# Attention and gated MLP on one Trainium2 core: the order of all operations from a table instead of a greedy scheduler

## The chip, the core and the metric

The kernel runs on one core of a Trainium2 chip. The core has a matrix engine (TensorE, PE in the rows), a vector engine (VectorE, DVE), an engine for functions of one tensor (ScalarE, ACT), a general one (GpSimd, POOL) and a sync engine (SyncE, SP), which here issues all DMA transfers. Each takes its own queue of instructions in order and waits at the front of it for semaphores of the others. Loads of weights into PE (PEld) overlap its matmuls. The metric is the device time of one execution in microseconds (us), the median over runs.

## What is computed

Causal attention for 4 batches of 12 heads (448 positions, 64 wide), whose output goes as x into a gated MLP with a spatial mix. All inputs are float32, some weights arrive as 64-bit numbers.

```python
scores = (q @ k.transpose(0, 1, 3, 2)) / np.sqrt(64)
scores = np.where(mask, -1e9, scores)            # causal
attn = np.exp(scores - scores.max(-1, keepdims=True))
attn = attn / (attn.sum(-1, keepdims=True) + 1e-9)
x = (attn @ v).transpose(0, 2, 1, 3).reshape(4, 448, 768)
h = np.maximum(x @ w_in, 0)                      # 768 -> 1024
u, v = h[..., :512], h[..., 512:]
v_n = (v - mean(v)) / np.sqrt(var(v) + 1e-6)
v_s = np.einsum('ts,bsd->btd', w_spatial, v_n) + b_spatial[None, :, None]
out = (u * v_s) @ w_out                          # 512 -> 768
```

## The kernel before

The kernel first writes down all its work as a list of 2517 operations (`Plan.add`), each with the engines that may run it and a time on each, what it reads and writes, and the buffers it needs. Then `Plan.run` decides engine by engine in which order they are issued. The operations are these.

Attention goes by pairs of heads, 24 pairs, six to a batch, numbered from 0. For each pair `load` brings q and k in and `qk_prepare` brings them into the form in which the head's 64 rows lie on partitions: for the first twelve pairs by PE transposes in float32 (`qk_turn`, L708, copies L729 and L731), for the others scaled, split into two 16-bit halves (L528 is the second half, by subtraction) and turned by a DMA transpose into qkT (L773, L784). Scores go into PSUM banks ps (L859 for the first ten pairs, L1005 for two, L1015 and L1016 later), DVE adds the mask and takes the maximum (L884, L1026), ACT the exponential (L894, L1038), DVE sums and reciprocals (L905, L1052, L1060). The weights e are turned by PE (L933, copied to et by L958 and L960) or, from pair 10 on, by DMA transposes (L1142). The product with the values is L1167, into the one bank px, and leaves it through ACT (L1184) and DVE (L1189) into xT.

The MLP (`ffn`) goes by batches, once six pairs are done. All its matmuls are in `chain` (L1396), in pieces of three. It makes the v half of h (L1462), its norm (L1470 to L1508), the u half (L1545, L1547), the spatial product (L1577), g = u times v_s, in two halves (L492 to L496 and L1417), and the output (evacuated into buffers o by L1613 and L1615, stored by L1625).

The weights are prepared in between: `prep_in` for w_in (L1236 and `from_double`), `prep_sp` for w_spatial, `prep_out` for w_out. `prep_out` takes eight loads (L1362) into the two buffers o, which later also hold outputs. From each load `from_double` assembles 32-bit numbers in three steps on DVE (L1202, L1208, L1213), and then a rounded copy (L494 or L496) and the rest (L1376) are written into wo.

What sets the order: each engine takes the ready operation with the smallest rank. The rank is a latest start, worked back from due times (`DUE`) and shifted by two tables of offsets (`LEAN` by part and engine, `NUDGE` by group). `WHERE` says which engine runs an operation that several could. Where PE has nothing ready in the first 46 us of the plan, a filler matmul is issued, L660, which multiplies a constant into the bank pf2:

```python
if op is None:
    if e == "PE" and self.warm and 1300 <= now < WARM:
        order.append((self.warm, e))
        busy[e] = pe_end = now + FILL
```

Of the kernel before, what the change touches and what calls it, by code (L numbers as in the profile page):

```python
# [57 lines left out]
)  # L58
NUDGE = (
# [5 lines left out]
)  # L65
LEAN = {
    (0, "DVE"): -1630, (0, "PE"): 330, (0, "POOL"): -3560, (0, "SP"): 1020, (1, "ACT"): 5410, (1, "DVE"): -1290, (1,
    "PE"): 1970, (1, "POOL"): -4890, (1, "SP"): -5940, (2, "ACT"): -3040, (2, "PE"): 6920, (2, "POOL"): 610, (2,
    "SP"): 5090, (3, "DVE"): 21930, (3, "PE"): 8670, (3, "POOL"): 4350, (3, "SP"): 4620, (4, "ACT"): -25990, (4,
    "DVE"): -4700, (4, "SP"): 6360, (5, "ACT"): 360, (5, "DVE"): 16860, (5, "PE"): 1330, (5, "POOL"): 1940, (6,  # L70
    "ACT"): -5080, (6, "DVE"): -1250, (6, "PE"): -2420, (6, "POOL"): 1170, (6, "SP"): -5620, (7, "ACT"): -5140, (7,
    "DVE"): 830, (7, "PE"): -10610, (7, "POOL"): -2630, (7, "SP"): -120, (8, "ACT"): 1470, (8, "DVE"): 1160, (8,
    "PE"): 4610, (8, "POOL"): 1070, (9, "DVE"): -1240, (9, "PE"): 1950, (9, "POOL"): 4140, (9, "SP"): 1390, (10,
    "ACT"): -1730, (10, "DVE"): -1120, (10, "PE"): 410, (11, "ACT"): 1330, (11, "PE"): -580, (11, "POOL"): -3820,
    (11, "SP"): 200, (12, "ACT"): 60, (12, "DVE"): -180, (12, "PE"): 6160, (12, "POOL"): -2020, (13, "ACT"): 3270,
    (13, "DVE"): 560, (13, "PE"): -950, (13, "POOL"): -3310, (13, "SP"): 4100, (14, "DVE"): 3280, (14, "POOL"):
    1600, (14, "SP"): 330, (15, "ACT"): 490, (15, "DVE"): -1430, (15, "POOL"): -1560, (15, "SP"): -430, (16, "ACT"):
    -1470, (16, "DVE"): -2030, (16, "POOL"): -1090, (16, "SP"): -4720, (17, "ACT"): 2080, (17, "DVE"): 2600, (17,
    "PE"): 1720, (17, "POOL"): 4210, (17, "SP"): -450, (18, "ACT"): -1950, (18, "DVE"): -6170, (18, "PE"): -1700,
    (18, "POOL"): -550, (18, "SP"): -14920, (19, "ACT"): 1850, (19, "SP"): -4980, (20, "ACT"): 4940, (20, "DVE"):  # L80
    480, (20, "POOL"): 880, (20, "SP"): -4390, (21, "DVE"): 2620, (21, "POOL"): 3170, (22, "ACT"): 13050, (22,
    "DVE"): 590, (22, "PE"): -10700, (22, "POOL"): 280, (22, "SP"): -11070, (23, "ACT"): 5360, (23, "DVE"): -840,
    (23, "POOL"): 2610, (23, "SP"): -330, (24, "DVE"): 2330, (24, "PE"): 430, (24, "POOL"): 4180, (24, "SP"): -2720,
    (25, "ACT"): -11200, (25, "DVE"): -2770, (26, "ACT"): -6170, (26, "DVE"): -2660, (26, "PE"): 200, (26, "POOL"):
# [225 lines left out]
def kernel(  # L310
# [278 lines left out]
    st = {}  # L589
# [1110 lines left out]
```

## Time and profile before

| | |
|---|---|
| time, median of 3 runs | 380.98 us (380.76 to 385.32) |
| the profiled execution's own time | 383.96 us |
| its span, first to last instruction | 382.2 us |
| what lies around the span | 1.76 us |
| PE busy, fillers included | 364.3 us, 95% |
| DVE / ACT / POOL busy | 298.1 / 259.8 / 147.2 us |
| granted clock of TensorE, mean | 0.989 |

Busy time is the time in which an engine executes. [...] In a row of the timeline the time in brackets is how long the engine was idle just before, and behind the arrow stands what ended it. An instruction's line in the rows is a line of the kernel before.

### The profile page before, as it was taken

The numbers are of one execution on the slowest core, as the hardware profiler recorded it, in microseconds if no ns is written. First come the engines' busy times: TensorE is split into PE (matmuls) and PEld (weight loads), VectorE is DVE, ScalarE is ACT, GpSimd is POOL, SyncE is SP. The second block draws the span as 40 slices with busy tenths as digits, with TensorE's granted clock in tenths as the row PEclk, the third lists the DMA queues.
The fourth block names the chain that finished last, engine by engine and source line by source line (L and its number), as shares of the span: only waits on it lengthen the run. The fifth ranks groups of instructions, "written<-read, shape, count | busy, mean of one in ns | idle before, by whom it ended". The sixth has DMA issues, their size and how long they took to land.

```text
span 382.2 us, 8138 instructions
## 1 busy us (share of the span) xinstructions
PE 364.3 (95%) x2621; PEld 233.3 (61%) x2621; DVE 298.1 (78%) x1152; ACT 259.8 (68%) x764; POOL 147.2 (39%) x208
## 2 busy tenths in 40 slices
PE   8999999899999999699998989999899999999995
PEld 6676654456445554576654548865455687555695
DVE  4998989899899999669887889889799988154210
ACT  1889997689989594379886794787785579142111
POOL 3111496258985522023596041413163310034410
PEclk9999999999999999889999999999999999999999
DMA  7999953563325999928999989989657678600022
GB/s 189 229 228 229 219 123 121 149 121 96 88 49 132 236 216 207 234 101 160 192 204 171 188 140 144 232 191 202 139 115 138 107 171 152 147 0 0 2 82 82
DMA packets 157964, 56.64 MB, mean 148 GB/s; under 512 B 151457, under 2 KB 153698, under 8 KB 157922
## 3 DMA queue, kind: packets, MB, share of 16 engines
q1 hardware_dynamic: 157922, 56.14, 70.9%
q8 instruction: 20, 0.33, 0.4%
q14 instruction: 22, 0.18, 0.1%
HBM read 26.76 MB, written 5.51 MB: 84 GB/s over the span
## 4 chain that ended last, share of the span: by engine, by line
PE 46%; DVE 20%; ACT 16%; DMA 12%; issue 3%; SPq 2%; ACTq 0%; DVEq 0%
PE pf L1396 26%; PE px L1167 5%; ACT ps L1038 5%; PE pf L660 5%; PE ps L859 3%; DMA et<-e 3%; DMA o<-in_moe_w_out_dram 3%; DVE ps L1026 3%; ACT e L494 3%; ACT junk L572 2%; PE ps L933 2%; DVE e L1127 2%; DVE ps L884 2%; PE ps L708 2%; PE ps L1015 2%
## 5 line engine op out<-in xcount | busy, mean ns | idle before, releaser
L1038 ACT ACTIVATE ps<-ps,sm 128x384 f32<-128x384 f32 (+4 forms) x98 | 45.4, 464 | 24.1 <-DVE sm L1026 17.3
L1396 PE MATMUL pf<-wi,xT 128*128 128x512 f16 (+1 forms) x360 | 59.8, 337 | 0.0
L1396 PE MATMUL pf<-xT,wi 128*128 128x448 f16 x288 | 59.0, 352 | 0.1
L1396 PE MATMUL pf<-wo,g 128*128 128x384 f32 x288 | 57.0, 351 | 1.6 <-ACT o L1613 1.3
L1396 PEld LDWEIGHTS pf<-wo,g 128*128 128x128 f32 x288 | 51.9, 196 | 4.3 <-ACT o L1613 1.4
L1127 DVE SCALAR_TENSOR_TENSOR e<-ps,sm,e 128x256 f16<-128x256 f32 (+4 forms) x98 | 45.2, 505 | 5.4 <-ACT e L494 5.2
L1396 PEld LDWEIGHTS <-wi 128*128 128x128 f16 x288 | 27.8, 99 | 24.9 <-issue 1.4
L496 POOL TENSOR_SCALAR e<-e,sm 128x384 f32<-128x384 f32 (+3 forms) x38 | 22.7, 606 | 52.1 <-DVE sm L905 14.7
L494 ACT ACTIVATE e<-ps,sm 128x384 f16<-128x384 f32 (+4 forms) x98 | 40.9, 515 | 2.6 <-DVE sm L1060 2.6
L1396 PEld LDWEIGHTS <-xT 128*128 128x128 f16 (+1 forms) x360 | 27.7, 103 | 23.1 <-issue 3.6
L1026 DVE CUSTOM_DVE_ANT_0 ps<-ps,mask,sc 128x384 f32<-128x384 f32 (+4 forms) x84 | 38.3, 507 | 4.1 <-PE ps L1016 3.8
L894 ACT ACTIVATE e<-ps,sm 128x128 f32<-128x128 f32 (+3 forms) x70 | 34.0, 497 | 6.3 <-DVE sm L884 4.3
L1396 PE MATMUL pf<-wst,vn 128*128 128x448 f16 (+1 forms) x176 | 36.1, 353 | 0.0
L1489 POOL TENSOR_TENSOR ln<-ln,mhalf 128x1 f32<-128x1 f32 (+1 forms) x16 | 9.2, 588 | 56.5 <-DVE ln L1481 42.4
L859 PE MATMUL ps<-qkT 64*128 64x128 f32 (+3 forms) x160 | 27.7, 445 | 0.9 <-ACT e L894 0.9
L1396 PEld LDWEIGHTS <-vn 128*128 128x128 f16 (+1 forms) x176 | 16.8, 98 | 16.2 <-issue 1.3
L884 DVE CUSTOM_DVE_ANT_0 ps<-ps,e 128x256 f32<-128x256 f32 (+2 forms) x60 | 24.2, 441 | 2.7 <-PE ps L859 2.5
L933 PE MATMUL ps<-ident,e 128*128 128x128 f32 x160 | 23.8, 279 | 1.3 <-DVE qkT L731 0.9
L1167 PE MATMUL px<-et,vs 128*64 128x448 f16 (+3 forms) x336 | 22.7, 276 | 1.9 <-DMA et<-e 1.8
L1016 PE MATMUL ps<-qkT 128*64 128x384 f16 (+4 forms) x168 | 21.9, 285 | 1.5 <-DMA qkT<-qkT 1.5
L933 PEld LDWEIGHTS ps<-ident,e 128*128 128x128 f32 x160 | 17.6, 141 | 9.1 <-issue 4.0
L528 POOL TENSOR_TENSOR qks<-qk,qks 112x512 f16<-112x512 f32 x15 | 17.8, 1200 | 13.8 <-ACT qks L494 13.6
(152 smaller groups left out, 755.2 us busy)
## 6 DMA issues: line engine op xcount, KB each, us to landing
wb<-in_moe_w_in_dram SPq DMA_DIRECT2D x12, 512.0 KB, 4.6
vnat<-in_v_dram SPq DMA_DIRECT2D x24, 192.0 KB, 4.2
out_dram<-o SPq DMA_DIRECT2D x12, 384.0 KB, 2.6
o<-in_moe_w_out_dram SPq DMA_DIRECT2D x8, 384.0 KB, 4.2
qk<-in_q_dram SPq DMA_DIRECT2D x24, 112.0 KB, 4.2
qk<-in_k_dram SPq DMA_DIRECT2D x24, 112.0 KB, 3.9
qk<-in_q_dram SPq DMA_DIRECT2D x12, 224.0 KB, 3.9
qk<-in_k_dram SPq DMA_DIRECT2D x12, 224.0 KB, 4.0
```

The lines of the kernel that those rows point to most:

```text
L494: nc.scalar.activation(out=dst, in_=src, func=AF.Copy, scale=scale)
L496: nc.gpsimd.tensor_scalar(out=dst, in0=src, scalar1=scale, scalar2=1.0, op0=ALU.mult, op1=ALU.mult)
L859: nc.tensor.matmul(out=at(bank)[r0:r0 + rn, o0:o0 + n], lhsT=flat32(t)[rows, q0:q0 + rn], rhs=k32(t)[rows, :n], start=True, stop=True, ski ...
L884: lambda e, ps=ps, n=n, u=u0 + u, sm=sm, o0=o0, h=h: nc.vector.tensor_tensor_reduce(out=at(ps)[:, o0:o0 + n], in0=at(ps)[:, o0:o0 + n], in ...
L894: lambda e, ps=ps, n=n, u=u0 + u, sm=sm, o0=o0, c=c: nc.scalar.activation(out=at(eb)[:, 128 * c:128 * c + n], in_=at(ps)[:, o0:o0 + n], fu ...
L933: nc.tensor.transpose(out=at(pt)[:, 128 * i:128 * i + 128], in_=e32(at(eb))[:, c0 + i, :], identity=ident)
L1016: nc.tensor.matmul(out=o, lhsT=w, rhs=qkT[:, 4 + x, :n], start=False, stop=True)
L1026: lambda e, ps=ps, n=n, u=u, sm=sm, o0=o0, m0=m0: nc.vector.tensor_tensor_reduce(out=at(ps)[:, o0:o0 + n], in0=at(ps)[:, o0:o0 + n], in1=m ...
L1038: nc.scalar.activation(out=dst, in_=src, func=AF.Exp, scale=-1.0, bias=at(sm)[:, u:u + 1], accum_out=at(sm)[:, 4 + u:5 + u],)
L1127: lambda e, part=part, src=src, sm=sm, u=u: nc.vector.scalar_tensor_tensor(out=part(1), in0=src(), scalar=at(sm)[:, 8 + u:9 + u], in1=part(0),
L1167: nc.tensor.matmul(out=at(px)[64 * h:64 * h + 64, 128 * j:S], lhsT=lhsT, rhs=rhs, start=(j == 0 and t == 0), stop=(j == 3 and t == (0 if t ...
L1396: nc.tensor.matmul(out=o, lhsT=a(), rhs=rhs, start=(n0 + n == 0), stop=(n0 + n == len(mms) - 1), skip_group_check=len(out_ap()) > 1,)
```

## The change

The scheduler's rules go (ranks, due times, `LEAN`, `NUDGE`, `SLACK`, the test for free buffers in turn). In their place stands `ORDER`, a table with the numbers of all 2517 operations in the order in which they are issued; the change's title says that it was found by moving single operations in the sequence. `WHERE`, the table of engines, is new as well. `Plan.run` walks through `ORDER` and gives each operation the next free buffer of its kind in the order of release; it still works out times from costs, but these decide only how many fillers are put in. The costs of DMA transfers are changed a little. The operations, what they need and the instructions of each are the same. From here on lines of code have moved up, by 26 to 42: the loads of w_out are L1327, assembling is L1170, L1176 and L1181, the copy to xT is L1157.

```diff
-DEEP = 5500
-EARLY, LAZY, REACH = 12490, 23190, 110
-SLACK = 120, 50, 20, 10, 0, 80
 WHERE = (
-    "DDDPPAAPPAPDPPPDDPPPAAAADAPPAAPADAAADDADDADADDPDADPDPPDDPPPPDPPDPPDPPDADPPAAPAADPDDAAAAAPPDDPADDDDPAPDAAAPPDDP"
...
+    "AADPPAADPAPDAPDPDAPDDAPPADAPAAPAPAPAAAPPAADPDDPAPAPDAAPADPDAPPPPAAPPDPADAPAAPPAAPDPDPAAAAPAAAAAAAAADAAAPPAADAA"
...
-DUE = (
...
-NUDGE = (
...
-LEAN = {
...
+ORDER = (
+    12, 1, 8, 3, 10, 9, 4, 0, 5, 11, 7, 6, 22, 73, 161, 2, 74, 103, 153, 13, 72, 15, 14, 71, 16, 97, 104, 154, 23,
...
+        for n in ORDER:
+            op = self.ops[n]
+            e = op.at_engine
+            waits = list(op.deps)
+            for b in op.bufs:
+                if b.slot is None:
+                    b.slot, b.before = free[b.kind].pop(0)
+                    left[b] = len(b.ops)
+                waits += b.before
+            start = max([busy[e]] + [d.end + self.delay(d, e) for d in waits])
+            if e == "SP":
+                start = max(start, ring - op.move[3])
...
+            if e == "PE":
+                if last not in (None, op.cls) and start - busy[e] < 1:
+                    start += SWITCH["afr".index(last)]
+                last = op.cls
+                if busy[e] < WARM and (2, []) in free["pf"]:
+                    now = max([busy[e], 2700] + [d.end + self.delay(d, e) if d.end else start for d in self.warm.deps])
+                    while now + (fill := FILL if now > 6000 else 2 * FILL) < start - 40:
                         order.append((self.warm, e))
...
+                        now += fill
...
-    LOAD = {"qk1": (490, 1150, 520), "qk2": (570, 1200, 1040), "v": (500, 1300, 890), "v64": (650, 1300, 500),
-            "w_in": (420, 1300, 1900), "w_sp": (400, 1300, 800), "b_sp": (400, 1300, 100), "w_out": (430, 1300, 1100)}
-    LOCAL = 580, 1300, 560
-    STORE = {128: (500, 1000, 970), 64: (580, 1000, 700)}
-    TURN = {16: (1860, 1100, 1500), 24: (3985, -700, 3300), 6: (1250, 700, 800), 2: (1200, 850, 300)}
+    LOAD = {"qk1": (490, 1150, 540, 4200), "qk2": (570, 1100, 1150, 3000), "v": (500, 1300, 850, 4200),
+            "v64": (650, 1200, 650, 4200), "w_in": (430, 1300, 1980, 4200), "w_sp": (400, 1300, 800, 4200),
+            "b_sp": (400, 1300, 100, 4200), "w_out": (430, 1300, 1400, 3400)}
+    LOCAL = 580, 1350, 400, 3000
+    STORE = {128: (500, 1000, 970, 3500), 64: (580, 1000, 850, 3500)}
+    TURN = {16: (1750, 850, 1850, 2000), 24: (3900, -600, 3300, 2800), 6: (1250, 400, 1100, 3000), 2: (1200, 750, 400, 3000)}
```

What the tables do is seen in the order of the instructions. On SP, before, around the last two of the eight loads of w_out (o0 and o1 are the two buffers they go to; et0 and e1 belong to pair 10, et1 and e0 to pair 11; qk1 and vnat0 are loads of later pairs):

```order
L1142 DMA_TRANSPOSE et0_94<-e1_93 128x24x128
L1362 DMA o0_110<-in_moe_w_out_dram 128x768
L1362 DMA o1_111<-in_moe_w_out_dram 128x768
L1142 DMA_TRANSPOSE et0_94<-e1_93 128x6x128
L1142 DMA_TRANSPOSE et0_94<-e1_93 128x2x128
L773 DMA_TRANSPOSE qkT1_85<-qks0_83 128x16x112
L680 DMA qk1_81<-in_q_dram 112x8x64
L1142 DMA_TRANSPOSE et1_95<-e0_92 128x2x128
L680 DMA qk1_81<-in_k_dram 112x8x64
L813 DMA vnat0_86<-in_v_dram 128x6x64 x3
L1362 DMA o0_110<-in_moe_w_out_dram 128x768
L1362 DMA o1_111<-in_moe_w_out_dram 128x768
```

And on SP after the change, at the same loads (here pair 10 uses et1 and e1):

```order
L1327 DMA o1_111<-in_moe_w_out_dram 128x768
L755 DMA qkT0_84<-qkT0_84 64x896
L646 DMA qk1_81<-in_k_dram 112x4x64
L783 DMA vnat2_88<-in_v_dram 64x6x64
L783 DMA vnat2_88<-in_v_dram 128x6x64
L1327 DMA o0_110<-in_moe_w_out_dram 128x768
L1110 DMA_TRANSPOSE et1_95<-e1_93 128x6x128
L653 DMA qk1_81<-in_k_dram 112x8x64
L1327 DMA o1_111<-in_moe_w_out_dram 128x768
L1110 DMA_TRANSPOSE et1_95<-e1_93 128x2x128
L1327 DMA o0_110<-in_moe_w_out_dram 128x768
L1110 DMA_TRANSPOSE et1_95<-e1_93 128x24x128
```

The last loads now stand among the three transposes of pair 10, where before they stood behind all of these, one of pair 11 and three loads of v; and the loads no longer go in pairs.

On DVE, before, at the last two rounds of assembling w_out (hv0 and hv1 receive the numbers; xT2 is the result of pair 10, on its way out of px; L1026 belongs to the softmax of later pairs). These are rows 516 to 525 of its queue:

```order
L1202 TENSOR_SCALAR hv0_112<-o0_110 128x384
L1189 SCALAR_TENSOR_TENSOR xT2_98<-px0_76,xT2_98 128x448
L1208 SCALAR_TENSOR_TENSOR hv0_112<-o0_110,hv0_112 128x384
L1202 TENSOR_SCALAR hv1_113<-o1_111 128x384
L1213 SCALAR_TENSOR_TENSOR hv0_112<-o0_110,hv0_112 128x384
L1208 SCALAR_TENSOR_TENSOR hv1_113<-o1_111,hv1_113 128x384
L1026 ISA ps3_75,sm5_122<-ps3_75,mask_62,sc0_123 128x256
L1026 ISA sm5_122 128x1
L1213 SCALAR_TENSOR_TENSOR hv1_113<-o1_111,hv1_113 128x384
L1376 TENSOR_TENSOR wo2_1652<-hv0_112,wo2_1652 128x384
```

On DVE after the change, the same two rounds (rows 476 to 484; L1020 and L1028 are sums and reciprocals of the softmax):

```order
L1170 TENSOR_SCALAR hv0_112<-o1_111 128x384
L518 TENSOR_SCALAR sc2_125<-sc2_125 128x1
L1176 SCALAR_TENSOR_TENSOR hv0_112<-o1_111,hv0_112 128x384
L1170 TENSOR_SCALAR hv1_113<-o0_110 128x384
L1028 RECIPROCAL sm5_122<-sm5_122 128x2
L1176 SCALAR_TENSOR_TENSOR hv1_113<-o0_110,hv1_113 128x384
L1020 TENSOR_SCALAR sm1_118<-sm1_118 128x1
L1181 SCALAR_TENSOR_TENSOR hv0_112<-o1_111,hv0_112 128x384
L1181 SCALAR_TENSOR_TENSOR hv1_113<-o0_110,hv1_113 128x384
```

The last round ends in row 484 instead of 524, and the xT copy of pair 10 is no longer queued between its steps; that of pair 9 follows in row 494.

## Rows read from the trace of the kernel before

**Rows 1.** Stage table: stretch, length, busy time and instructions, granted clock, DMA share.

```profile
core 0: us, PE busy (x) PEld busy (x) DVE busy (x) ACT busy (x) POOL busy (x), PEclk, DMA share, GB/s
0.00:40.00 40.00, 38.83 (x299) 27.70 (x301) 32.76 (x131) 28.68 (x90) 7.99 (x30) 1.00 0.98 222
40.00:140.00 100.00, 96.91 (x639) 54.45 (x637) 92.75 (x367) 85.31 (x265) 63.96 (x87) 1.00 0.61 135
140.00:180.00 40.00, 35.78 (x241) 24.89 (x242) 31.52 (x126) 26.14 (x79) 8.45 (x10) 0.91 0.84 177
180.00:280.00 100.00, 94.69 (x774) 60.33 (x773) 85.95 (x348) 75.37 (x214) 40.33 (x51) 1.00 0.97 182
280.00:360.00 80.00, 79.86 (x572) 48.60 (x571) 51.67 (x179) 40.76 (x114) 23.77 (x30) 1.00 0.47 92
360.00:383.00 23.00, 18.20 (x105) 17.29 (x102) 3.45 (x6) 3.52 (x8) 2.72 (x3) 0.95 0.20 68
sum 383.00, PE 364.28 PEld 233.26 DVE 298.09 ACT 259.78 POOL 147.22; mean PE 60.71 PEld 38.88 DVE 49.68 ACT 43.30 POOL 24.54
```

**Rows 2.** Stage table of the fillers alone (L660): PE, PEld, clock, DMA.

```profile
0.00:40.00 40.00, 20.80 (x143) 14.48 (x143) 1.00 0.98 222
40.00:140.00 100.00, 0.77 (x4) 0.39 (x4) 1.00 0.61 135
```

**Rows 3.** Timelines of SP, DVE and PE between 150 and 168 us: start, length, instruction, idle before.

```profile
151.71 1.64 SPq L1362 DMA_DIRECT2D o<-in_moe_w_out_dram  x2
...
157.71 0.36 DVE L1202 TENSOR_SCALAR hv<-o 128x384 int32<-128x384 int32 x1 [3.66 <-DMA o<-in_moe_w_out_dram]
157.99 0.62 DVE L1189 SCALAR_TENSOR_TENSOR xT<-px,xT 128x448 f16<-128x448 f32 x1
...
153.11 2.88 PE L1396 MATMUL pf<-wo,g 128*128 128x384 f32 x15
...
158.66 0.48 PE L581 MATMUL px<-sc,ones 112*128 112x2 f32 x2 [2.17 <-DVE xT L1189]
160.43 6.83 PE L1396 MATMUL pf<-wo,g 128*128 128x384 f32 x24 [1.29 <-ACT o L1613]
```

**Rows 4.** Timeline of all engines, 0 to 16 us: PE's first rows.

```profile
1.10 4.56 PE L660 MATMUL pf<-ones 128*128 128x256 f16 x22 [1.10 <-DVE ones L598]
...
5.51 0.55 PE L708 MATMUL ps<-ident,qk 112*128 112x112 f32 x4
...
5.89 0.82 PE L660 MATMUL pf<-ones 128*128 128x256 f16 x6
...
6.55 0.55 PE L708 MATMUL ps<-ident,qk 112*128 112x112 f32 x4
...
8.07 1.61 PE L859 MATMUL ps<-qkT 64*128 64x128 f32 x12
```

**Rows 5.** Timeline of PE, 96 to 99 us: chain pieces and attention work by turns.

```profile
96.03 0.82 PE L1396 MATMUL pf<-wi,xT 128*128 128x512 f16 x3
96.78 0.92 PE L859 MATMUL ps<-qkT 64*128 64x384 f32 x4
97.62 0.82 PE L1396 MATMUL pf<-wi,xT 128*128 128x512 f16 x3
98.28 1.30 PE L1396 MATMUL pf<-xT,wi 128*128 128x448 f16 x6
```

**Rows 6.** Groups of DVE instructions by line: count, busy us, mean ns, idle before.

```profile
L731 DVE COPY qkT<-ps 128x448 f32<-128x448 f32 (+1 forms) x15 | 9.2, 620 | 2.5 <-PE ps L708 2.3
...
L1208 DVE SCALAR_TENSOR_TENSOR hv<-o,hv 128x384 int32<-128x384 int32 x8 | 4.2, 551 | 0.0
...
L1202 DVE TENSOR_SCALAR hv<-o 128x384 int32<-128x384 int32 x8 | 2.8, 353 | 3.9 <-DMA o<-in_moe_w_out_dram 3.9
...
L528 DVE TENSOR_TENSOR qks<-qk,qks 112x512 f16<-112x512 f32 x9 | 7.1, 799 | 0.4 <-ACT qks L494 0.4
...
L528 DVE TENSOR_TENSOR wi<-wa,wi 128x512 f16<-128x512 f32 x6 | 4.4, 738 | 0.0
...
L1417 DVE TENSOR_TENSOR g<-u,g 128x384 fp32r<-128x384 f32 x8 | 4.3, 552 | 0.0
```

**Rows 7.** Timeline of all engines, 374 to 383 us: the last copies.

```profile
377.72 1.07 ACT L1613 ACTIVATE o<-pf 128x384 f32<-128x384 f32 x2 [4.19 <-PE pf L1396]
```

**Rows 8.** Costliest groups on the page: the products with the values, from px.

```profile
L1167 PE MATMUL px<-et,vs 128*64 128x448 f16 (+3 forms) x336 | 22.7, 276 | 1.9 <-DMA et<-e 1.8
```

More of the change, by code (lines that the diff above doesn't have):

```diff
@@ L140, in add @@
         deps.discard(op)
+        op.n, op.end = len(self.ops), 0
         op.deps = sorted(deps, key=lambda o: o.n)
-        op.bufs = list(dict.fromkeys(k[0] for k in list(reads) + list(writes) if isinstance(k[0], Buf)))
+        op.bufs = list(dict.fromkeys(k[0] for k in (*reads, *writes) if isinstance(k[0], Buf)))
         for b in op.bufs:
-            b.left += 1
-            if b.turn is None:
-                b.turn = self.turns[b.kind]
-                self.turns[b.kind] += 1
+            b.ops.append(op)
         self.ops.append(op)
@@ L157, in delay, with run @@
         return tail + CROSS[op.at_engine][ENGINES.index(to)]
-    def place(self):
+    def run(self):
         where = iter(WHERE)
-        dues, groups = {}, {}
         for op in self.ops:
@@ new lines, in run @@
+        free = {k: [(n, []) for n in range(c)] for k, c in self.slots.items()}
+        left = {}
+        busy = dict(FIRST)
+        order, ring, last = [], 0.0, None
+        pool_end = dve_end = 0.0
+        for n in ORDER:
[10 more added lines that the diff above has]
+                start = max(start, ring - op.move[3])
+            if e in op.lock:
+                start = max(start, pool_end)
+            if e == "POOL":
+                start = max(start, dve_end)
+            if e == "PE":
[5 more added lines that the diff above has]
+                    while now + (fill := FILL if now > 6000 else 2 * FILL) < start - 40:
+                        order.append((self.warm, e))
+                        now += fill
+            op.at = start
+            op.end = busy[e] = start + op.eng[e]
+            if e == "POOL":
+                pool_end = op.end + TAIL[e]
+            if e in op.lock:
+                dve_end = op.end + TAIL[e]
+            if e == "SP":
+                op.end = ring = max(ring, op.end + op.move[1]) + op.move[2]
+            order.append((op, e))
+            for b in op.bufs:
+                left[b] -= 1
+                if not left[b]:
+                    free[b.kind].append((b.slot, b.ops))
@@ L306, in run @@
+        self.length = max(op.end for op in self.ops)
         return order
@@ L574, in square_sum, with total @@
         writes = [wkey] + ([(j, 0)] if junk else reads)
-        plan.add({"ACT": c_act(n, "S", 1)}, fn, (reads if junk else []) + list(also), writes, rank)
-    def total(acc, rows, n, reads, rank):
+        plan.add({"ACT": c_act(n, "S", 1)}, fn, (reads if junk else []) + list(also), writes)
+    def total(acc, rows, n, reads):
         ps = Buf("px")
@@ L583, in total @@
             ),
-            reads + [const_key("ones")], [(ps, 0)], rank,
+            reads + [const_key("ones")], [(ps, 0)],
         )
@@ L595, in early @@
         def early(cost, fn, writes, reads=(), eng="DVE"):
-            plan.add({eng: cost}, fn, list(reads), [const_key(w) for w in writes], -10)
+            plan.add({eng: cost}, fn, list(reads), [const_key(w) for w in writes])
         early(120, lambda e: nc.vector.memset(ones, 1.0), ["ones"])
@@ L1215, in third, with prep_in @@
             )
-        plan.add({"DVE": c_fast(n)}, first, reads, [key], rank, lock=LOCK)
-        plan.add({"DVE": c_both(n)}, second, reads, [key], rank, lock=LOCK)
-        plan.add({"DVE": c_both(n)}, third, reads, [key], rank, lock=LOCK)
-    def prep_in(part, rank, gate=()):
+        plan.add({"DVE": c_fast(n)}, first, reads, [key], lock=LOCK)
+        plan.add({"DVE": c_both(n)}, second, reads, [key], lock=LOCK)
+        plan.add({"DVE": c_both(n)}, third, reads, [key], lock=LOCK)
+    def prep_in(part, gate=()):
         c0 = DH * (1 - part)
@@ L1385, with chain @@
     TERMS = [(0, 0), (0, 1), (1, 0)]
-    def chain(ps, out_ap, mms, cost, keys, due, cls="f"):
-        plan.group = due
+    def chain(ps, out_ap, mms, cost, keys, cls="f"):
         for n0 in range(0, len(mms), 3):
@@ L1640 @@
     for p in range(NPAIR):
-        plan.part = p
         if p + 2 < NPAIR:
```

461 lines of the change are left out of this document (132 added, 329 removed), and 140 rows, old and new, of tables (DUE, NUDGE, ORDER).

## The prediction

> **What bounds the kernel now.** I read the stage table first: the busy time of each engine in six stretches [rows 1]. TensorE (PE) is busy nearly everywhere, so the question is how much of that is work. The same table for the filler matmuls alone gives 20.80 us in the first 40 us [rows 2]; they multiply a constant into a scratch bank and compute nothing. So the useful share of the first stretch is 38.83 - 20.80 = 18.0 us of 40. PE without useful work is then, by stage [rows 1, 2]: 0 to 40 us 22.0; 40 to 140 us 100 - 96.91 + 0.8 of fillers = 3.9; 140 to 180 us 40 - 35.78 = 4.2; 180 to 280 us 5.3; 280 to 360 us 0.1; from there to the end of the span at 382.2 us 22.2 - 18.20 = 4.0. That is 39.5 us. The change touches no arithmetic, so all that it can win from idle time is in this list, and PE's last 95 us hold next to none of it. The second engine is VectorE (DVE): 92.75 of 100 us in the second stretch, 85.95 in the fourth [rows 1].
>
> The place with a name is 140 to 180 us, where the granted clock is also down to 0.91 [rows 1]. The timeline there reads as one story [rows 3]. The last two loads of w_out are issued by the sync engine (SP) at 151.71 us. DVE, which takes its queue in order, stands idle 3.66 us until 157.71 for that data (L1202), and the copy of an attention result out of PSUM (xT, L1189) is queued right behind. PE waits 2.17 us for that copy, then 1.29 us for an output buffer, then runs 24 matmuls in 6.83 us. [...] The stall costs 2.2 + 1.3 + 2.2 = 5.7 us.
>
> **The change, part by part.** The 2517 operations and what each needs are the same; their order in each queue is new, some change engine, and fillers fall from 147 to 88 (counted in the two orders). I sum against the profiled execution, 383.96 us; the median of the three runs is 380.98, and I carry the difference over unchanged.
>
> *w_out earlier.* In the two excerpts of the order, SP's last w_out loads move from behind a whole set of transposes of one attention pair, and the first of the next, into the middle of the former's. On DVE the last assembling step moves from row 524, behind the xT copy of pair 10, to row 484, ahead of that of pair 9: 40 rows. At 367 instructions in 100 us or 126 in 40 [rows 1], that is 11 to 13 us. On PE the first chains that use the parts prepared last stand behind 913 useful matmuls before and behind 898 after, 15 x 0.19 = 2.9 us sooner. So the data come some 12 us sooner for a need that comes 3 us sooner, against a wait of 3.66. I take 5.5 of the 5.7 us. Ends: 0, if the loads are held up in SP's queue as long as before, and 5.7.
>
> *The start.* Fillers stand only where the planner sees PE idle. Of the 59 that go, 15 are from the first block (22 before, 7 after), which ran while the first loads came in [rows 4] and whose loss frees nothing. The other 44, at 0.82/6 = 0.137 us each [rows 4], covered 6.0 us. If the new order really fills that time with work, 6.0 us come off; if PE merely waits instead, 0. DVE has 32.76 of 40 us busy there and DMA 0.98 [rows 1], so I take less than half: 2.5.
>
> The clock speaks against this. The first 22 fillers take 4.56 us, 0.207 each, and later ones 0.137 [rows 4]: PE ran at the lower level until that block was nearly over, and the first transposes already ran at the higher one. By the order alone the useful start (two groups of four transposes, 0.55 each, and twelve score matmuls, 1.61 [rows 4]) could run at half speed after seven fillers, +2.7 us. [...] I leave the 2.7 out of the sum, since twice before a group of transposes six fillers ran first, 0.66 us each time (5.89 to 6.55) [rows 4], while the new order has the first two groups back to back, and since DVE and the loads set the pace of that stretch more than PE.
>
> *Fewer changes of kind on PE.* Counted over PE's queue, it turns from a feed-forward chain to attention work 57 times before and 39 after. A chain piece of three 512-column matmuls took 0.75 us from its start to the next piece when attention followed (96.03 to 96.78) and 0.66 when a chain followed (97.62 to 98.28) [rows 5]: 0.09 each, times 18, 1.6 us. The opposite turn shows no such price; ends 0 and 3.2.
>
> *Work off DVE.* Subtractions for qks and wi on DVE go from 15 to 8 (7 at 0.78: 5.4 us), those for g from 8 to 3 (2.8), copies of turned q and k from 15 to 11 (2.5) [rows 6]: some 10.7 us go to GpSimd (POOL) and ScalarE (ACT). POOL has the room, 63.96 of 100 us in its fullest stretch [rows 1]. This only pays where PE waits behind DVE: at most the 3.9 and 5.3 us of the second and fourth stretches, at least 0. DVE is fullest in the second; I take half of 3.9, 2.
>
> *The end.* Before, two copies stand behind PE's last matmuls on one engine, 1.07 us [rows 7]; after, one, so 0.5 comes off. The end of the queue is otherwise the same chains and the same store.
>
> *New waits.* Attention results wait for transposes through DMA, 1.8 us in total [rows 8]. The PE work put between a pair's last scores and its use is about as before for most pairs, less for a few and more for others. An order without slack will meet some of these in new places: I take -2, once more what they cost now; ends 0 and -6, three times.
>
> Sum: 5.5 + 2.5 + 1.6 + 2 + 0.5 - 2 = 10.1 us. On 383.96 that is 373.9; on the median 380.98 it is 370.9, 2.7% less.
>
> **The rivals.** *The stall moves to DVE (within 2%).* The eight rounds of assembling w_out are 8 x (0.35 + 0.55 + 0.55) = 11.6 us of DVE work [rows 6], the third step like the second. They move into the stretch where DVE is fullest, and softmax of pairs 8 to 10 would be later by that, less what DVE sheds there (10.7 x 100/320 = 3.3): PE waits 8 us more, 378.9. For it: DVE 92.75 of 100. Against it: the xT copies of pairs 8 to 10 stand within 11 rows of where they stood on DVE, so it was other work that gave way.
>
> *The gain is only the named stall (within 2%).* The start, the relief and the end give 0 and the new waits cost 4: 5.5 + 1.6 - 4 = 3.1, 377.9. For it: the start is full of DMA (0.98), and a rearrangement can't bring loads earlier. Against it: the turns on PE and the last copy are sure.
>
> *The clock stays down (slower).* If the fillers that go are what held the granted clock at 1.00 through the first 40 us, the 18.0 us of useful work take 36, and the result is 370.9 + 18.0 = 388.9, 2.1% slower. For it: one idle spell of 2.17 and 1.29 us at 158 us was followed by a slow stretch [rows 3]. It decides only if nearly all of those 40 us are slow; ten slow us cost less than 4.5 and leave the result faster than before. Against it: 81 fillers remain behind the first block, and work moves up. [...]
>
> **How the numbers follow.** About 2% is what a measurement of this kernel can tell from no change: under 373.4 us is faster, over 388.6 slower. Chances: the forecast and its neighbours down to 360 us, 0.58; the stall on DVE 0.22; only the named stall 0.14; the clock or some other collapse 0.06. Faster 0.58, same 0.36, slower 0.06. Time 370.9 us. Range: all terms at their good ends and no new wait give 5.7 + 6.0 + 3.2 + 9.2 + 0.5 = 24.6, 356, which needs everything at once; I put the low end at 363. The high end takes in both rivals within 2%: 380. Together some 8 in 10.
>
> **What the profile of the changed kernel would show.** w_out: no wait of DVE L1202's counterpart on DMA above 1 us, and a granted clock of 1.00 in 140 to 180 us. Start: useful PE work (busy less fillers) in the first 40 us above 20 us rather than 18.0. Relief: DVE's total down from 298.09 to about 287, POOL's and ACT's up. Turns: PE's busy total less the fillers, 342.7 now, lower by one or two us. New waits: PE waiting for transposed et or qkT by more than 1.8 us in total. The prediction is wrong if the first 40 us show a granted clock below 1.00 in useful work, or if PE's idle time in 40 to 140 us rises above 6 us.

## The result and the profile after

The changed kernel takes 369.07 us (368.48 to 369.34, 4 runs) against 382.58 us before (380.76 to 385.32, 4 runs): ratio 0.9639, 95% interval 0.9568 to 0.9711, so 3.6% faster, 13.5 us. The forecast was 370.9 us, 2.7% less. Its profiled execution took 368.89 us with a span of 367.2, against 383.96 and 382.2; the sum of the prediction, 10.1 us, has to answer to these 15.1.

The stage table of the changed kernel answers to [rows 1] (columns as there):

```profile
0.00:40.00 40.00, 35.51 (x245) 22.43 (x247) 32.56 (x142) 31.49 (x104) 15.15 (x42) 1.00 0.92 217
40.00:140.00 100.00, 98.48 (x660) 56.32 (x655) 92.50 (x364) 94.69 (x280) 49.03 (x67) 1.00 0.68 156
140.00:180.00 40.00, 39.60 (x334) 28.36 (x333) 35.69 (x144) 32.67 (x94) 18.39 (x23) 1.00 0.93 174
180.00:280.00 100.00, 96.92 (x769) 61.33 (x768) 80.69 (x343) 81.39 (x231) 44.52 (x54) 1.00 0.90 168
280.00:345.00 65.00, 64.48 (x458) 40.64 (x457) 38.52 (x128) 30.40 (x81) 17.02 (x22) 1.00 0.48 107
345.00:368.00 23.00, 18.22 (x105) 17.27 (x102) 5.86 (x12) 1.36 (x3) 3.38 (x4) 0.97 0.21 70
sum 368.00, PE 353.21 PEld 226.34 DVE 285.82 ACT 272.00 POOL 147.49; mean PE 58.87 PEld 37.72 DVE 47.64 ACT 45.33 POOL 24.58
```

And the fillers alone, to [rows 2]:

```profile
0.00:40.00 40.00, 14.28 (x88) 8.39 (x88) 1.00 0.92 217
```

From 140 to 180 us the granted clock (a share of the full one; the lower level is recorded as 0.50, before from 158.8 to 165.6 us) is 1.00 (0.91 before) and PE is busy 39.60 of 40 us. PE's busy time less the fillers is 353.21 - 14.28 = 338.9 us, 3.8 less than before (342.7); the other 11.2 of the 15.0 us of span are idle time and fillers.

The timelines of SP, DVE and PE at the place of [rows 3] (here o0 and o1 are filled for the last time):

```profile
133.49 0.53 SPq L1327 DMA_DIRECT2D o<-in_moe_w_out_dram  x1
...
137.98 0.35 DVE L1170 TENSOR_SCALAR hv<-o 128x384 int32<-128x384 int32 x1
...
142.31 1.89 PE L1360 MATMUL pf<-wo,g 128*128 128x384 f32 x9
...
144.54 1.60 PE L1135 MATMUL px<-et,vs 128*64 128x448 f16 x24
...
147.75 6.49 PE L1360 MATMUL pf<-wo,g 128*128 128x384 f32 x36
```

The last load is issued at 133.5 us instead of 153.0 (the second of the two in the first row of [rows 3]), DVE does not wait for it, and 36 chain matmuls take 6.49 us, 0.18 each, where 24 took 6.83.

PE's first rows, against [rows 4]:

```profile
2.75 1.46 PE L634 MATMUL pf<-ones 128*128 128x256 f16 x6 [2.75 <-DVE ones L571]
4.87 1.72 PE L680 MATMUL ps<-ident,qk 112*128 112x112 f32 x8 [0.66 <-DMA qk<-in_q_dram]
6.39 0.85 PE L634 MATMUL pf<-ones 128*128 128x256 f16 x3
7.23 2.15 PE L829 MATMUL ps<-qkT 64*128 64x128 f32 x12
```

Eight transposes take 1.72 us, 0.215 each (0.138 before), twelve scores 2.15 (1.61 before). The start is slower per matmul than it was. The column of the granted clock says 1.00 for this stretch in both kernels, but the trace's record of the clock has its first entry only at 8.45 us (at 5.21 before), and the column counts what lies ahead of it as 1.00; there the matmul times are the evidence.

From the groups by line (count, busy us, mean ns, idle before), against [rows 8] and [rows 6]:

```profile
L1135 PE MATMUL px<-et,vs 128*64 128x448 f16 (+3 forms) x336 | 22.7, 275 | 0.1
...
L1170 DVE TENSOR_SCALAR hv<-o 128x384 int32<-128x384 int32 x8 | 3.1, 392 | 0.4 <-POOL vn L1482 0.4
```

To see where the 15 us come from I read progress instead of busy time. PE's useful operations and their planned costs are the same in both kernels, 330.8 us in all. For each kernel the table gives the time (us from the span's start, in its profiled execution) at which PE has so much of this work of its queue behind it, on a straight line between the starts of two operations; the last column is at 328.4.

```
work done      20     30     60     90    100    120    130    180    240   328
before        39.8   51.3   85.0  116.9  127.3  149.8  166.9  220.4  285.8  375.6
after         39.6   49.8   82.2  114.1  124.2  144.2  154.3  207.5  270.5  360.6
last_loads    39.4   50.9   83.3  117.1  127.5  150.0  161.7  216.0  283.9  373.5
hold_one      40.0   50.2   82.0  113.9  124.0  148.2  159.6  211.7  275.4  365.7
wout_back     39.5   49.6   82.5  114.4  124.5  148.3  166.4  219.6  283.4  373.7
relief_back   39.6   49.8   85.2  117.4  127.5  148.3  159.3  212.6  276.0  366.4
turns         39.5   49.7   82.9  116.5  127.0  147.8  158.1  212.0  277.5  368.6
a65b          39.1   49.1   81.5  117.2  127.6  150.8  167.8  221.8  284.9  374.5
no_fill       41.3   51.7   83.9  115.8  125.9  145.9  156.1  208.3  271.1  360.5
start18       38.9   49.1   81.2  113.2  123.2  143.2  153.4  205.5  268.3  358.4
```

After is ahead of before by 0.2 us at 20, 1.5 at 30, 2.9 at 60, 3.1 at 100, 5.6 at 120, 12.5 at 130, 12.8 at 180, 15.2 at 240 and 15.0 at the end (differences of the unrounded times). The stall of w_out, between 120 and 130, is 6.9 of the 15.

### The profile page after: what moved, and what is told of

It is laid out like the page before. It is cut to its first block, busy times and chain, and to the rows that moved or that the text cites. A ratio compares the mean times of both kernels' runs of the same rounds, so it can differ in the third digit from the quotient of the medians.

```text
span 367.2 us, 7993 instructions
## 1 busy us (share of the span) xinstructions
PE 353.2 (96%) x2562; PEld 226.3 (62%) x2562; DVE 285.8 (78%) x1129; ACT 272.0 (74%) x786; POOL 147.5 (40%) x208
## 3 DMA queue, kind: packets, MB, share of 16 engines
HBM read 26.76 MB, written 5.51 MB: 88 GB/s over the span
## 5 line engine op out<-in xcount | busy, mean ns | idle before, releaser
L1006 ACT ACTIVATE ps<-ps,sm 128x256 f32<-128x256 f32 (+4 forms) x98 | 45.3, 463 | 15.2 <-DVE sm L994 12.6
L1360 PE MATMUL pf<-wo,g 128*128 128x384 f32 x288 | 53.5, 339 | 0.3 <-ACT u L1505 0.3
L1095 DVE SCALAR_TENSOR_TENSOR e<-ps,sm,e 128x384 f16<-128x384 f32 (+4 forms) x98 | 46.4, 503 | 8.5 <-ACT e L467 8.4
L1360 PEld LDWEIGHTS pf<-wo,g 128*128 128x128 f32 x288 | 49.9, 188 | 2.0 <-issue 1.1
L467 ACT ACTIVATE e<-ps,sm 128x384 f16<-128x384 f32 (+4 forms) x98 | 44.5, 507 | 7.3 <-DVE sm L1028 5.8
L994 DVE CUSTOM_DVE_ANT_0 ps<-ps,mask,sc 128x384 f32<-128x384 f32 (+4 forms) x84 | 40.0, 506 | 5.6 <-PE ps L984 4.8
L469 POOL TENSOR_SCALAR e<-e,sm 128x384 f32<-128x384 f32 (+3 forms) x37 | 19.9, 548 | 41.8 <-DVE sm L883 27.4
L854 DVE CUSTOM_DVE_ANT_0 ps<-ps,e 128x128 f32<-128x128 f32 (+2 forms) x60 | 24.7, 443 | 3.1 <-PE ps L829 2.5
L501 POOL TENSOR_TENSOR qks<-qk,qks 112x512 f16<-112x512 f32 x19 | 22.1, 1176 | 8.1 <-DVE qks L465 2.7
L1135 PEld LDWEIGHTS <-vs 128*64 128x64 f16 (+1 forms) x336 | 16.3, 109 | 9.0 <-issue 2.1
```

The costliest lines, as they stand in the source:

```text
L467: nc.scalar.activation(out=dst, in_=src, func=AF.Copy, scale=scale)
L501: lambda e: HANDLE[e].tensor_tensor(out=dst_l(), in0=src(), in1=dst_h(), op=ALU.subtract),
L854: lambda e, ps=ps, n=n, u=u0 + u, sm=sm, o0=o0, h=h: nc.vector.tensor_tensor_reduce(out=at(ps)[:, o0:o0 + n], in0=at(ps)[:, o0:o0 + n], in ...
L994: lambda e, ps=ps, n=n, u=u, sm=sm, o0=o0, m0=m0: nc.vector.tensor_tensor_reduce(out=at(ps)[:, o0:o0 + n], in0=at(ps)[:, o0:o0 + n], in1=m ...
L1006: nc.scalar.activation(out=dst, in_=src, func=AF.Exp, scale=-1.0, bias=at(sm)[:, u:u + 1], accum_out=at(sm)[:, 4 + u:5 + u],)
L1095: lambda e, part=part, src=src, sm=sm, u=u: nc.vector.scalar_tensor_tensor(out=part(1), in0=src(), scalar=at(sm)[:, 8 + u:9 + u], in1=part(0),
```

## The experiments

Each is the kernel before or the changed one with one thing altered. Instructions and fillers are otherwise as in that kernel, and so are buffers, except in wout_only, wout_back and a65b, where the moved operations take some of them in another turn. Line numbers are those of the changed kernel. The ratio of each is to the kernel before on the same chip; the changed kernel stands at 0.9639 (0.9568 to 0.9711), an interval that those of hold_one, relief_back and turns don't touch. Differences "by the medians" are between runs on different chips.

| run | alters | time, us | ratio to before (95%) |
|---|---|---|---|
| wout_only | before | 393.67 | 1.0306 (1.0267 to 1.0344) |
| last_loads | before | 379.86 | 0.9901 (0.9864 to 0.9938) |
| wout_back | after | 383.25 | 1.0012 (0.9979 to 1.0045) |
| hold_one | after | 374.46 | 0.9790 (0.9761 to 0.9820) |
| where_only | before | 401.21 | 1.0515 (1.0475 to 1.0555) |
| relief_only | before | 387.93 | 1.0083 (1.0046 to 1.0119) |
| relief_back | after | 374.58 | 0.9774 (0.9745 to 0.9802) |
| turns | after | 377.82 | 0.9826 (0.9782 to 0.9870) |
| a65b | both | 382.87 | 1.0012 (0.9987 to 1.0037) |
| no_fill | after | 369.00 | 0.9634 (0.9603 to 0.9666) |
| start18 | after | 367.12 | 0.9594 (0.9554 to 0.9633) |
| better | after | 367.48 | 0.9566 (0.9523 to 0.9609) |

### Where w_out stands

```diff
 # wout_only: the table is the order of before, with operations 473 to 520 moved
 # wout_back: the table is the order of after, with operations 473 to 520 moved
-    each of the 48 operations of prep_out at its own place
+    each at the amount of useful PE work at which the other kernel has it
```

> The order, the engines and the fillers of the kernel before; only the 48 operations that prepare w_out (loads, assembling, the two copies) stand at the place, counted in useful PE work, that they have after the change. Theory A (the stall on the last loads is about half of the gain, and its removal stands by itself): 5.5 to 7 us less than before, ratio about 0.983; no wait of DVE L1170 on w_out, granted clock 1.00 in 140 to 180 us. Rival B (the stall moves to DVE, as in the prediction: the work needs the room that the rest of the change makes): less than 2 us gained, ratio 0.995 or more, and PE waits for DVE between 90 and 130 us in its place.

It is 3.1% slower, which neither theory had. DVE and PE, timelines of wout_only:

```profile
125.73 0.36 DVE L1170 TENSOR_SCALAR hv<-o 128x384 int32<-128x384 int32 x1 [4.95 <-DMA o<-in_moe_w_out_dram]
...
130.38 1.01 PE L680 MATMUL ps<-ident,qk 112*128 112x112 f32 x4 [7.45 <-DVE e L1095]
```

DVE's step now stands right behind the load that it needs, since a load can only be issued when a buffer o is free (SP issued it when DVE had emptied that buffer, 4.9 us before it landed). DVE waits 4.95 us with the weights e of attention queued behind, PE 7.45 us for those, and the granted clock is 0.83 from 120 to 140 us, 0.86 and 0.88 in the next two stretches of 20 us. It is rival B's mechanism at a size of its own, and part of it is my way of grafting: places counted in PE work do not keep loads and steps apart. The run says what a badly placed load costs, not what the term is worth.

> The changed kernel with only these 48 operations put back to the places, counted in useful PE work, that they had before. Theory A: the stall comes back with its slow clock, 6 to 7.5 us more than after the change, ratio to before about 0.98, granted clock under 0.95 in 135 to 180 us. Rival B: about 2 us more than after at most, because the new order has room elsewhere and PE has other work in its queue while DVE waits.

The whole gain goes. Timeline of PE, wout_back:

```profile
152.10 1.82 PE L1360 MATMUL pf<-wo,g 128*128 128x384 f32 x9
156.78 0.69 PE L1360 MATMUL pf<-wo,g 128*128 128x384 f32 x1 [2.87 <-POOL wo L469]
158.62 5.15 PE L1360 MATMUL pf<-wo,g 128*128 128x384 f32 x17 [1.15 <-POOL wo L1341]
```

PE waits for w_out itself, then runs 17 chain matmuls at 0.30 us each (granted clock 0.90 from 140 to 160 us and 0.93 from 160 to 180, 1.00 in the changed kernel). In the table it keeps up with after to 100 (124.5 against 124.2) and is 12.1 us behind at 130. Theory A has the sign; 14 us is twice what it said. The same doubt about grafting holds, so two smaller edits followed.

```diff
 # last_loads, SP's queue in the order of before
+DMA o_110<-in_moe_w_out_dram 128x768
+DMA o_111<-in_moe_w_out_dram 128x768
 DMA qk_81<-in_k_dram 112x8x64
 DMA vnat_86<-in_v_dram 128x6x64 x3
-DMA o_110<-in_moe_w_out_dram 128x768
-DMA o_111<-in_moe_w_out_dram 128x768
 # hold_one, SP's queue in the order of after
-DMA o_110<-in_moe_w_out_dram 128x768
 DMA_TRANSPOSE et_95<-e_93 128x24x128
+DMA o_110<-in_moe_w_out_dram 128x768
```

> The kernel before, with nothing moved but the last two loads of w_out, which go on SP's queue ahead of one load of k and three of v instead of behind them: four issues, some 2.9 us sooner, by the times of the profile before. Every other engine has the same instructions in the same order. Theory A (DVE's wait for these loads costs PE 2.2 us, then 1.3, then 2.2 of slow clock): DVE's wait shrinks from 3.66 to under 1 us, PE's wait for the xT copy goes, the granted clock stays at 1.00 in 150 to 170 us, 4 to 6 us less than before, ratio about 0.987. Rival B (the next late thing takes its place, since PE stands right behind the assembled w_out in the order of before): 0 to 2 us less, ratio 0.995 or more, PE waiting for wo instead.

1.0% less, 3.8 us by the ratio. Timelines of SP and PE, last_loads:

```profile
149.13 1.00 SPq L1327 DMA_DIRECT2D o<-in_moe_w_out_dram  x2
...
156.83 4.44 PE L1360 MATMUL pf<-wo,g 128*128 128x384 f32 x24
162.82 1.62 PE L1135 MATMUL px<-et,vs 128*64 128x448 f16 x24 [1.56 <-DMA et<-e]
```

The 24 matmuls that took 6.83 us take 4.44, behind no wait: the stall of [rows 3] is gone, and the table has it 5.2 us ahead of before at 130. Some is given back: PE's waits for turned weights, of which the last row is one, grow from 1.8 [rows 8] to 2.7 us in total, and 4.4 us are left at 180. Another 2.5 go between 180 and 240, where PE's wait for qkT is 2.1 us instead of 1.5 and a stretch at a lower clock follows (0.57 granted from 267 to 271 us, 1.00 before). The profiled execution ends 2.1 us ahead, the median 3.8 by the ratio. Theory A at the place itself, just short of its range in the end.

> The changed kernel with one row of one queue changed: the load of w_out that SP issues last stands behind the largest of the three transposes of pair 10 instead of ahead of it, which is where before all late loads stood. By the trace of the changed kernel SP issues it 5.4 us later (138.9 instead of 133.5), the data come at about 143, and DVE's step for it stands at 138.0. Theory A (the place of these loads in SP's queue is the stall): DVE stands some 5 us at L1170, PE, which has 2.4 us between the last assembled part and its use, loses 2 to 5 us, 371 to 374 us, ratio to before up by 0.005 to 0.013. Rival B (the new order has other work everywhere, and the stall only hurt in the old one): within 1 us of the changed kernel. Rival C (as with the 48 operations put back): 10 us or more above the changed kernel, because softmax is queued behind the waiting DVE and a slow stretch of PE follows.

1.5 points of ratio above the changed kernel, 5.4 us by the medians, for one row of one queue. Timelines of DVE and PE, hold_one:

```profile
141.96 0.36 DVE L1170 TENSOR_SCALAR hv<-o 128x384 int32<-128x384 int32 x1 [4.08 <-DMA o<-in_moe_w_out_dram]
...
144.97 0.62 PE L1360 MATMUL pf<-wo,g 128*128 128x384 f32 x2 [2.52 <-DVE sm L1020]
146.41 1.80 PE L1360 MATMUL pf<-wo,g 128*128 128x384 f32 x7 [0.83 <-POOL g L1380]
...
148.88 2.58 PE L1135 MATMUL px<-et,vs 128*64 128x448 f16 x24
```

The same three parts as in [rows 3]: DVE waits 4.1 us, PE 2.5 and 0.8, and then runs slowly (24 products with v in 2.58 us instead of 1.60; granted clock 0.96 from 140 to 180 us instead of 1.00). The progress table shows 4.0 us lost by 120, 5.3 by 130 and 5.1 at the end. Theory A in mechanism, a little above its range (371 to 374 us).

### Work off DVE, and the table of engines

```diff
 # where_only: the order of before
-WHERE = (the 445 letters of before)
+WHERE = (the 445 letters of after; 246 differ)
 # relief_back: the order of after; relief_only: the order of before
 # seven subtractions of scale_split and five of gated
-    on POOL (relief_back) / on DVE (relief_only)
+    on DVE (relief_back) / on POOL (relief_only)
```

> The order and the fillers of before, with the table of engines of after: some 10.7 us of work leave DVE for POOL and ACT, nothing changes place in the sequence. Theory A (relief of DVE as in the prediction, half of PE's idle time in the second stretch): 2 us less than before, ratio 0.995. Rival E (DVE is the true limit of 40 to 280 us): 6 us or more less, 0.984 or under. Rival F (a table of engines is worth something only with its order, since the work meets other queues): the same or slower by up to 2 per cent, with PE waiting for POOL or ACT where it waited for DVE.

5.2% slower, although DVE has 6.4 us less to do (291.7 against 298.1). What PE waits for between 20 and 140 us, where_only (us in total, times, longest):

```profile
PE ps L829 <- ACT e L864: 1.9, 2, 1.7
PE ps L680 <- ACT e L864: 1.3, 2, 0.7
PE ps L973 <- ACT et L927: 1.0, 1, 1.0
PE ps L903 <- POOL e L469: 1.0, 1, 1.0
```

Rival F, beyond its 2%: PE waits for ACT and POOL in many small pieces, and is busy 88.2 of the 100 us from 40 to 140 instead of 96.9.

> The changed kernel with seven subtractions for halves of w_in and q, k and five for g, which it runs on POOL, put back on DVE at the same places of the sequence: some 8 us of work back on DVE between 60 and 210 us. Theory A (the relief of DVE is worth about 2 us, half of PE's idle time in the second stretch): 1 to 4 us more than the changed kernel, ratio to before about 0.97. Rival D (DVE is the true limit up to 280 us): 6 us or more above the changed kernel. Rival E (idle time of DVE takes it in, or these operations are faster on DVE and so earlier): the same time as the changed kernel within 1 us.

> The kernel before, with the same twelve subtractions on POOL that the changed kernel runs there (seven for halves of w_in and q, k, five for g), everything at its old place in the sequence. Theory A (the relief stands by itself, the term of the prediction): 1 to 4 us less than before, ratio 0.99 to 0.997. Rival B (the relief is worth what it is in the changed kernel, about 5.5 us, in either order): ratio 0.986. Rival F (in an order that was not made for it, a subtraction that takes 1.0 to 1.2 us on POOL against 0.55 to 0.78 on DVE is only later for the next): the same or up to 4 us more than before.

Relief_back is 5.5 us above the changed kernel by the medians, relief_only 0.8% above before. The stretch of 40 to 140 us in the stage table, relief_back and then relief_only:

```profile
40.00:140.00 100.00, 96.25 (x643) 55.10 (x639) 93.70 (x360) 91.75 (x271) 41.29 (x60) 1.00 0.66 150
```

```profile
40.00:140.00 100.00, 94.87 (x620) 52.82 (x619) 88.54 (x352) 82.51 (x254) 66.20 (x91) 0.98 0.56 129
```

In relief_only DVE falls from 92.75 to 88.54 us, and PE falls with it, from 96.91 to 94.87: less on DVE, and PE idle longer. The trace shows where: five of the moved subtractions run on POOL between 86.8 and 100.4 us, 1.15 us each, POOL's copy into wb (part of w_spatial) starts at 107.45 us instead of 105.29, DVE's copy xT stands behind DVE's use of wb, and PE waits 2.2 us for it until 114.2 us, a wait that before does not have; the granted clock is at its lower level from 114.3 to 117.7 us (0.98 over the stretch of the row, 1.00 before). In relief_back PE has 96.25 instead of 98.48. So this relief is worth something only in the order that was made with it; theory A fails in both directions (5.5 where 1 to 4 was expected, a loss where a gain was), rival D (6 or more) isn't reached in the one, rival F holds for the other.

### Turns on PE

```diff
 # turns: PE's queue in the order of after, at 23 places
 chain piece
-chain piece
 attention piece
+chain piece
 attention piece
```

> The changed kernel, with 23 pieces of feed-forward chains on PE changed in place with the attention piece behind them, so that PE turns from chain to attention 62 times instead of 39; the queues of all other engines are the same to the row. Theory A (a turn costs 0.09 us, and the 18 turns that the change saves are worth 1.6): some 23 times 0.09, 2.1 us more than the changed kernel, ratio to before up by 0.005; in the trace a three-piece of 512 columns takes 0.09 us longer where attention follows. Rival C (the price is hidden in waits of PE that are there anyway): the same time within 0.5 us. Rival D (what matters is which result comes sooner, not the turns): a change of either sign above 3 us.

It costs 8.7 us by the medians and 8.0 in the table, where 23 times 0.09 is 2.1. From the trace the price itself is right for some turns: between starts, a piece of three 448-column matmuls takes 0.57 us before another chain piece (median of 132 in the changed kernel) and 0.66 or more before scores or products with v (5); before transposes on PE or the small sums it takes 0.57 as well in five cases of seven. Turns of the dear kind are 35 before, 22 in the changed kernel and 39 in this run, so 17 more, or 1.5 us. PE's busy time grows by 4.0 us (353.2 to 357.2) and its idle time within the span by 3.9 (375.1 - 357.2 = 17.9 against 367.2 - 353.2 = 14.0). Rival D: half is waiting. My reading, which no run isolates, is that a result comes 0.6 us later or is asked for 0.6 us sooner, in an order in which most results are just in time.

### The start, the fillers and the clock

> Up to 65 us of useful PE work (some 80 us of time) the order and the engines of the changed kernel, behind that the operations left in the order and on the engines of before. Theory A (the start and the first stretch of mixed work hold some 3 us of the gain): 2 to 4 us less than before, ratio about 0.992, and the wait for w_out unchanged. Rival C (the gain at the start was the large term): 6 us or more less than before, ratio 0.984 or under. Rival D (the early gain is lost again at the w_out wait, which is set by the loads): no difference.

Ahead of before by 3.5 us at 60, it is 0.3 behind at 90: behind the seam PE is busy 18.86 of 20 us from 80 to 100 and 18.07 from 100 to 120, where before had 19.78 and 19.64, presumably since the order of before does not fit what the other has left undone. Rival D's outcome, but by the seam and not by the w_out wait; inconclusive on the size of the early gain.

```diff
 # no_fill
-WARM, FILL = 46000, 107
+WARM, FILL = 0, 107
 # start18 (better has this too); operation 0, the constant, also goes first in ORDER
-                        order.append((self.warm, e))
+                        order += [(self.warm, e)] * (1 if any(x == e for _, x in order) else 13)
```

> The changed kernel without any of its 88 filler matmuls. Theory A (the fillers stand only where PE is idle; what they are worth is the clock): the granted clock falls below 1.00 in parts of the first 40 us, and the useful work of that stretch, some 20 us at full clock, takes up to 5 us longer in those parts of it that PE paces; 1 to 5 us more than the changed kernel. Rival C (the start is paced by loads, DVE and ACT, whatever the clock): within 1 us of the changed kernel. Rival F (the clock stays down through the first 40 us, as in the prediction's slow case): 10 us or more above it.

The same time, without one filler. The stretch of 30 to 40 us and PE's first rows, no_fill:

```profile
30.00:40.00 10.00, 7.38 (x33) 4.12 (x29) 8.39 (x32) 9.30 (x31) 4.15 (x6) 0.70 1.15 261
```

```profile
4.59 1.73 PE L680 MATMUL ps<-ident,qk 112*128 112x112 f32 x8 [4.59 <-DMA qk<-in_q_dram]
6.95 2.93 PE L829 MATMUL ps<-qkT 64*128 64x128 f32 x12 [0.63 <-ACT qkT L701]
```

The clock does fall (0.70 granted), and PE is 1.7 us behind the changed kernel at 20 and 1.8 at 130, but level at the end. Theory A for the clock, rival C for the time. Of the 1.8 us, 0.8 are regained at one wait of PE, for the sums of a block of v (0.8 us here, 1.6 in the changed kernel); how the rest comes back between 130 and the end isn't settled.

> The changed kernel with 18 filler matmuls instead of 6 at PE's start, and the constant that they multiply written first on DVE, so that they can run from 1.1 to 4.8 us, while PE has nothing else. Theory A (the changed kernel runs its first eight transposes at the lower clock, 0.215 us each against 0.138 before, and its first twelve scores in 2.15 us against 1.61): both come back to the shorter times, the chain of the start is 0.5 to 1.2 us shorter, ratio to before about 0.002 to 0.003 below that of the changed kernel. Rival C (the loads of the first q and k and DVE set the pace of the start anyway): PE's matmuls are shorter but the time is the same within 0.3 us.

Timeline of PE, start18:

```profile
1.10 4.02 PE L634 MATMUL pf<-ones 128*128 128x256 f16 x18 [1.10 <-DVE ones L571]
4.92 1.70 PE L680 MATMUL ps<-ident,qk 112*128 112x112 f32 x8
...
7.25 1.57 PE L829 MATMUL ps<-qkT 64*128 64x128 f32 x12 [0.22 <-ACT qkT L701]
```

The scores are back to the shorter time (1.57 us, 1.61 before), the transposes not (1.70 for eight, 1.72 in the changed kernel): theory A for half of it. The profile is 0.7 us ahead of the changed kernel at 20, 0.9 at 130 and 2.0 at 180, where a wait of PE for the sums of a block of v (1.6 us at 190.9) didn't occur. About 2 us faster than the changed kernel by the medians; the intervals of the two ratios overlap.

> The kernel with 18 fillers at its start, and besides one pair of small matmuls of PE (the sums of a block of v, L554) put behind the four score pieces and a chain that stand behind it, since in the changed kernel PE waits 1.6 us for them at 190.9 us. Theory A (the wait is PE's alone): about 1 us below the kernel with 18 fillers where its execution has that wait, ratio to before 0.956 to 0.960. Rival C (that wait was gone already with the earlier start, in whose profile it is absent): the same as the kernel with 18 fillers, about 367 us.

```diff
 # better: PE's queue, besides the edit of start18
-total (L554), for the sums of a block of v
 four score pieces and four of a chain
+total (L554), for the sums of a block of v
```

The same as start18, 367.48 against 367.12 us: rival C. Both are faster than before by 4%.

## Why the prediction came out as it did

*What bounds the kernel* was right: the list of PE's idle time held the gain. Of 15.0 us of span 3.8 came from PE's busy time and 11.2 from idle time and fillers. How the 3.8 divide isn't shown: 1.6 for 18 turns and 2.2 for the slow matmuls would make them up, but the first transposes and scores took 1.1 more than before. The list was too long, though: rows of fillers and of useful matmuls overlap, and the useful rows alone are busy 22.4 of the first 40 us before, not 18.0.

*w_out earlier, 5.5 of 5.7 us*: right, in mechanism and size. The stage itself gave 6.9 us; undone by one row it cost 5.4, and two loads moved past four others in the order of before gave 5.2 at the place and 3.8 in the end. That the data would come 12 us sooner was too little: the last load is issued 19.5 us sooner. The lower end, loads held up in SP's queue, is what hold_one is. The last 2.2 of the 5.7 are read from [rows 3]: at 2.88/15 = 0.19 us each 24 matmuls are 4.6 us, they took 6.83 with the granted clock at 0.50 until 165.6 us, and in last_loads they take 4.44. The sign announced for it held: no wait for w_out, clock 1.00.

*The start, 2.5 us*: mis-sized, and the step that failed is "if the new order really fills that time with work". After 20 us of useful work the changed kernel is 0.2 us ahead. The sign announced, useful PE time above 20 us in the first 40, came out at 35.51 - 14.28 = 21.2, but proves nothing: matmuls at the lower clock are busy longer (24 of one kind 6.83 us in [rows 3], 5.2 us of that at 0.50, against 4.44 at 1.00 in last_loads), and by the useful rows alone it was 22.4 before already and is 25.4 now, for the same progress. The 1.5 us at 30 and 2.9 at 60 came later. In the changed kernel the fillers cover nothing (no_fill: 369.00 us without them, 369.07 with).

*The clock at the start*: the 2.7 us that were left out came to 0.6 on the transposes and 0.5 on the scores. They were my estimate for eight transposes and twelve scores at half speed; measured are 0.215 against 0.138 us for a transpose, behind 6 and 22 fillers, and 2.15 against 1.61 us for the twelve scores, 1.1 us together, 0.3% of the span. Leaving them out cost little: start18, where the clock rose at 6.68 us instead of 8.45, is 0.7 us ahead at 20 and 0.9 at 130, and no_fill, with the same time, bears out the reason given for it, that PE does not pace that stretch (which of loads and DVE does, no run separates). The sign of being wrong, useful work of the first 40 us below a clock of 1.00, did come: eight transposes and the first eight of twelve score matmuls started ahead of the rise at 8.45 us. It was set too sharp, for it cost about 1 us.

*Fewer turns, 1.6 us*: the price per turn is confirmed for turns into scores and products with v, of which 13 went (1.2 us), and not for those into transposes. The run called turns shows that it can't be taken out of its order: 23 of them cost 8.7.

*Work off DVE, 2 us*: the step that failed is taking relief as a gain by itself, at least 0. DVE's total fell to 285.8, as said (287), but ACT took the work (259.8 to 272.0), POOL did not (147.2 to 147.5). In the old order the same relief is a loss of 0.8%, in the new one its undoing costs 5.5 us.

*The end, 0.5 us*: nothing. PE's last matmul ends 4.0 us ahead of the span's end in both; one of the two copies before had run beside the last matmuls.

*New waits, -2 us*: a term with the wrong sign. The wait for turned et is 0.1 us instead of 1.9 [rows 8], with qkT 1.1 us where more than 1.8 was announced; the one new wait of size is 1.6 us for the sums of v. As I read it, an order found by trying single moves is not only dense, it has also moved what would have waited. The sum was 5 us too small. By the progress table the gain is 6.9 us at the stall, where the sum had 5.5, and 2.7 between 20 and 60, 2.5 between 100 and 120 and 2.4 between 180 and 240, where the other terms made 4.6 together. In the last of these stretches PE's waits for turned weights fell from 1.3 to 0.1 us and those for qkT from 1.5 to 0.6; which terms the other two belong to no run separates.

*The base.* 10.1 us taken from 380.98 gave 370.9, close to 369.07; but the kernel before has medians of 382.6 to 384.5 us in the later comparisons. The three runs that I summed against were on the low side, and by this luck about half of what the sum lacked is hidden. In per cent the forecast is 2.7 against 3.6.

*The rivals.* The stall did not move to DVE here, but wout_only and hold_one show that it was a matter of a row; only the named stall would have been 5 to 7 us; the clock stayed up once it had risen (1.00 from 8.45 to 366.85 us), and where it didn't (no_fill, 0.70 from 30 to 40 us) it cost nothing that lasted (369.00 us).

## What to carry over

Where engines take their queues in order, look for the load whose place in the queue of DMA issues comes last before a stage needs it: one row there was worth 5.4 us here, where twelve subtractions less on the busy engine were a loss in the old order. The gain of a reordering is not a sum over its parts, so try a part both alone in the old order and undone in the new; where the two differ, as they did here, part of it belongs to the order around it. Compare two orders by the time at which the same useful work is done, not by busy time, which counts slow matmuls and fillers as well.

## What was not expected of the hardware

Eighteen fillers (1.10 to 5.1 us) left the next eight transposes at 0.21 us each, while 22 (to 5.7) before were followed by transposes of 0.138. The trace's record of the granted clock shows the step: its first entry, at 1.00, begins at 5.21 us before, ahead of the first transposes (5.51), and at 6.68 us in start18, just behind the eight (4.92 to 6.62), though PE was busy from 1.10 us on in both. In the changed kernel it begins at 8.45 us and in no_fill at 10.14. Why the step came 1.5 us later in start18 than before no run shows. And in no_fill a stretch at the lower level from 34.0 to 40.9 us (0.70 granted from 30 to 40, 0.96 from 40 to 50), besides the late step, was not seen in the time at all (369.00 us against 369.07).
